# One ring of four PSUM banks, and loads, conversions and products moved, in attention with two MLPs

## The chip, the cores and the metric

The kernel runs on one core of one Trainium2 chip. The metric is the time of one execution in device microseconds, the median of several runs. TensorE (PE) multiplies, VectorE (DVE), ScalarE (ACT) and GpSimd (POOL) work on tiles in SBUF, and the first two of these also read and write PSUM, where TensorE leaves its products. SyncE (SP) issues DMA transfers. Every engine works through its own list of instructions in order and waits where an input is not there yet.

## The reference

```python
def _attn_ref(x, state):                    # x (8, 8, 512, 64), state (8, 8, 32, 64)
    scores = scale * np.matmul(x, state.transpose(0, 1, 3, 2))
    a = softmax(scores); xread = np.matmul(a, state)
    scores2 = scale * np.matmul(state, x.transpose(0, 1, 3, 2))
    a2 = softmax(scores2); sread = np.matmul(a2, x)
    return np.concatenate([xread, sread], axis=2)

x = attn_out.transpose(0, 2, 1, 3).reshape(8 * 544, 512)
h = x @ w_in;  x = (np.maximum(h, 0.0) + alpha * np.minimum(h, 0.0)) @ w_out   # 512 -> 2048 -> 512
h = x @ w2_in; x = (h - np.tanh(h)) @ w2_out                                   # 512 -> 2048 -> 512
```

The softmax is written out here as one word. The weights arrive as 64-bit floats. All products are to be of about single precision.

## The kernel before, in words

**Precision.** A number is kept as two parts of type `fp32r`, a high one and the rest, and each product is made of three matmuls (`TERMS`: high by high, high by low, low by high). The 64-bit weights of the first MLP are turned into such pairs on the chip by a conversion in 32 jobs (`jobs`), each of 128 rows by 512 columns. A job (f, 0) is two slices of 128 columns of `w_in`, and (f, 1) a slice of `w_out`. It passes through steps `conv_load`, `conv_a`, `conv_b`, `conv_s`, `conv_c` and `conv_d`, each a fixed number of ticks after the one before: ScalarE takes the words apart (L112, L124) and makes the high part, VectorE clamps, shifts and masks (L115, L117, L120), GpSimd adds and subtracts (L167, L173, L176).

**Blocks and visits.** The first MLP goes through the tokens in blocks: eight batches of 512 and one of 256 for all state rows. A visit (i, f) is one slice f of 128 of the 2048 hidden units for block i. It makes the hidden product (`emit_h`, tile `ps_h`), the activation (`act_a`, `act_b`: ScalarE, VectorE, ScalarE, VectorE), and then the output product of the visit before (`emit_o`, four accumulators in the pool `ps_acc`). The visits run (0, 0) to (0, 7), then (1, 0) to (1, 15), then (0, 8) to (0, 15), then the blocks from 2 on, with 16 each; the state rows' block (8) comes next to last, before block 7. The first visits run while the weights are still being converted.

**What stands between.** A table, `plan`, puts everything else at one of five places in a visit: `early` (after the hidden product), `gap`, `mid` (after the activation), `late` (after the output product), `end`. Such entries are the attention of the next blocks in steps `s0` to `s6` (transposes `ps_xt`, scores `ps_s`, their softmax, the second transposes `ps_e`, reads `ps_r`, `ps_w`), the turning of states (`ps_st`), the conversion (`conv_step_a`, `conv_step_b`, set by `halves`), and, for blocks from 1 on, the state products (`project_one`, tile `ps_p`).

**State products.** From block 1 on the attention's read is not made as such; the state rows are multiplied by `w_in` ahead, and the hidden product multiplies that by the attention weights. `project_one(b, q, g, p)` does it for two neighbouring blocks at once, for a quarter q of the hidden units, half g of the heads and pair p. It copies the two parts to SBUF, from there to DRAM (`pw_dram`, L416), and `load_parts` (L423) brings each block's rows back as `PW`, for which block 1 uses room in the last piece of `WO`, which is not converted until later.

**PSUM.** There are eight banks: four for `ps_acc`, two for `ps_h` and two for `ps_a`, from which all other tiles come. A pool gives out the bank that was freed first, and its new user waits until the old one has been read.

**The second MLP** is a fast matrix scheme with seven products per pair of slices. An `octet` makes 14 products of six matmuls for two slices (L820); their copies and sums go through small tiles, and `store_g` (L808) sends the results to DRAM. `tasks` lists the block pairs and the order of the weight chunks, of which `load_chunk` (L714) fetches seven at a time and `load_pair` (L726) the next pair's inputs. Banks come from `bank()`, in turn over all eight. The second half (L1001) multiplies the results by the output weights.

The DMA issues mostly stand in SP's list, in the order in which the code calls them.

Of the kernel before, what the change touches and what calls it, by code (L numbers as in the profile page):

```python
# [22 lines left out]
P = 128  # L23
# [12 lines left out]
def attention_and_two_mlps(ctx, tc, x, state, w1_in, w1_out, alpha, w2_in, w2_out, out):  # L36
# [22 lines left out]
    ps_acc = ctx.enter_context(tc.tile_pool(name="ps_acc", bufs=4, space=PSUM))  # L59
    ps_h = ctx.enter_context(tc.tile_pool(name="ps_h", bufs=2, space=PSUM))  # L60
    ps_a = ctx.enter_context(tc.tile_pool(name="ps_a", bufs=2, space=PSUM))
    dram = ctx.enter_context(tc.tile_pool(name="dram", bufs=1, space=DRAM))
# [63 lines left out]

    jobs = [(f, half) for f in range(NF // 2) for half in range(2)]
    jobs += [(f, 0) for f in range(8, 12)] + [(8, 1)] + [(f, 0) for f in range(12, 16)] + [(f, 1) for f in range(9, NF)]
    raws, words, low, loaded = {}, {}, {}, set()
# [179 lines left out]

    def queue(b, g):  # L310
        return nc.scalar if (b, g) == (0, 1) else nc.sync

    def load_state(b, g, tag="sg"):
        sg = work.tile([P, D], F32, tag=tag, name=f"{tag}{b}_{g}", bufs=4)
        queue(b, g).dma_start(out=sg, in_=state[b, g * GH:(g + 1) * GH].rearrange("h n d -> (h n) d"))
        SG[(b, g) if tag == "sg" else (b, g, 0)] = sg

    def load_x(b, g):
        if b < 2:
            load_state(b, g)  # L320
        if b == 0:
            if g == 0:
                xraw[b] = w_outs.tile([P, 2 * NC * GH * D], F32, tag="wo", name="xr0")
            n = NC * GH * D
            t = xraw[b][:, g * n:(g + 1) * n].rearrange("p (c h d) -> p c h d", c=NC, h=GH)
        else:
            t = work.tile([P, NC, GH, D], F32, tag="xr", name=f"xr{b}_{g}")
        for h in range(GH):
            queue(b, g).dma_start(out=t[:, :, h, :],
                              in_=x[b, g * GH + h].rearrange("(p c) d -> p c d", c=NC))  # L330
        xraw[b, g] = t
# [43 lines left out]
    def parts_tile(b, q, g):  # L375
        if b == 1 and q < 2:
            open_wo(NF // FQ - 1)
            t = WO[NF // FQ - 1][:, :, 2 * q + g, :]
        else:
            t = work.tile([P, 2, DM], F32R, tag="raw", name="pw", bufs=4)  # L380
        PW[b, q, g] = [t[:, 0], t[:, 1]]
        return t
# [5 lines left out]
    def staged(b):  # L388
# [6 lines left out]
        n_staged[0] += 1  # L395
        if k < 8:
            open_wi(NF // FQ - 1)
            return tuple(WI[NF // FQ - 1][:, i, k % NCC, :] for i in range(2))
# [4 lines left out]
    def project_one(b, q, g, p):  # L403
# [5 lines left out]
        for k, (i, j) in enumerate(TERMS):  # L409
            nc.tensor.matmul(ps, lhsT=SN[b, g][:, i, cols, :].rearrange("p k m -> p (k m)"),  # L410
                             rhs=WI[q][:, j, g * NP + p, :], start=(k == 0), stop=(k == 2))
        hi, lo = staged(b)
        nc.scalar.copy(hi[d], ps)
        nc.vector.tensor_tensor(lo[d], ps, hi[d].bitcast(F32), op=ALU.subtract)
        for k, t in enumerate((hi, lo)):
            nc.sync.dma_start(out=pw_dram[b, q, g][p, k, d], in_=t[d].bitcast(F32))  # L416
# [178 lines left out]
    def emit_h(blk, n, f):  # L595
        ps = ps_h.tile([P, S], F32, tag="h", name="ps_h")
        if 0 < blk < B:
# [122 lines left out]
    RX, XT = {}, {}  # L720

    def load_pair(u):
        for k in range(2):
            for m in range(2):
                t = slots.get([P, 2, S], F32, f"rx{u}_{k}{m}")
                nc.sync.dma_start(out=t, in_=y_dram[2 * u + m][2 * k:2 * k + 2].rearrange("c p n -> p c n"))  # L726
                RX[u, k, m] = t

# [69 lines left out]
    def bank(shape=(P, S)):  # L798

        pool, tag = ((ps_a, "a"), (ps_a, "a"), *[(ps_acc, "acc")] * 4, (ps_h, "h"), (ps_h, "h"))[turn[0] % 8]  # L800
        turn[0] += 1
        return pool.tile(list(shape), F32, tag=tag, name="ps_m")
# [232 lines left out]
    def timetable(i, a, c):  # L1035

        if i == 0:
            when = dict(s0=(2, "late"), s1=(3, "early"), s2=(3, "late"), s2t=(3, "end"), s2b=(3, "end"), s3=(3, "end"),
                        s3x=(4, "gap"), s3b=(4, "late"), s4=(4, "end"), s4m=(4, "end"), s4t=(4, "end"), s4b=(5, "gap"),
                        s5=(5, "early"), s6=6)  # L1040
            then = dict(s0=(5, "late"), s1=(6, "early"), s2=6, s2t=(6, "late"), s2b=(6, "late"), s3=(6, "late"),
                        s3x=(6, "end"), s3b=7, s4=(7, "early"), s4m=(7, "early"), s4t=(7, "gap"), s4b=7, s5=(7, "late"),
                        s6=(NF, "late"))
        else:
# [5 lines left out]
            start = 7 if i + 2 < B else 5  # L1050
            when, then = (table(0), table(start)) if i > 1 else (table(9), table(8 + NF))
        for g, table in ((a, when), (c, then)):
# [9 lines left out]
    with tc.manual_schedule():  # L1062
# [16 lines left out]
        for f in range(NF // 2):  # L1079
            halves(0, f, "early", "gap")  # L1080
        for f in range(11):
            if f in (2, 3, 4):
                halves(1, f, "early", "gap", "mid", "end")
            else:
                halves(1, f, "gap", "end")
        at(0, 0, "gap", a.s2b)
        at(0, 0, "late", c.s2b)
        at(0, 1, "mid", a.s3b, c.s3b)
# [4 lines left out]
        turns = [(0, 1, 0, (0, "mid"), (1, "late")), (0, 2, 0, (1, "late"), (2, "early")),  # L1093
                 (0, 1, 1, (3, "mid"), (4, "early")), (0, 2, 1, (3, "late"), (4, "late"))]
        for i in (2, 4, 6):
# [17 lines left out]
        todo = [(1, q, g) for q in range(NF // FQ) for g in range(NG)]  # L1113
        places = [(0, 4), (0, 5), (1, 0), (1, 1), (1, 3), (1, 4), (1, 6), (1, 7)]
        todo += [(b, q, g) for b in (3, 5, 7) for g in range(NG) for q in range(NF // FQ)]
# [15 lines left out]
        for i, (blk, n) in enumerate(seq):  # L1131
            if i + 1 < B:
                timetable(i, a, attention(i + 1, 1))
                if i + 2 < B:
                    a = attention(i + 2, 0)
                    for j, f in (((1, 2), (1, 4)), ((0, 9), (0, 15)))[i] if i < 2 else ((i, 6), (i, 13)):
                        at(j, f, "late", load_next_x)
# [85 lines left out]
        for i in range(7):  # L1223
            load_chunk(1, i)
        at_visit = 0
        for k, (u, os) in enumerate(tasks):
            coming = tasks[k + 1][0] if k + 1 < len(tasks) else None
# [99 lines left out]
```

## Time and profile before

| | |
|---|---|
| median of 3 runs | 1509.73 us (1509.43 to 1513.57) |
| the profiled execution | 1510.44 us, span of its instructions 1508.6 us |
| TensorE busy | 1422.1 us, 94% |
| VectorE busy | 991.6 us, 66% |
| ScalarE, GpSimd busy | 729.7 us (48%), 532.1 us (35%) |

Shares are means over stages that are limited by different things: conversion, attention and first visits up to 209 us, the rest of the first MLP up to 815 us, the second MLP's first half up to 1196 us and its second half. Times in rows count from the span's start.

### The profile page before, as it was taken

The numbers are of one execution on the slowest core, as the hardware profiler recorded it, in microseconds if no ns is written. First come the engines' busy times: TensorE is split into PE (matmuls) and PEld (weight loads), VectorE is DVE, ScalarE is ACT, GpSimd is POOL, SyncE is SP. The second block draws the span as 40 slices with busy tenths as digits, with TensorE's granted clock in tenths as the row PEclk, the third lists the DMA queues.
The fourth block names the chain that finished last, engine by engine and source line by source line (L and its number), as shares of the span: only waits on it lengthen the run. The fifth ranks groups of instructions, "written<-read, shape, count | busy, mean of one in ns | idle before, by whom it ended". The sixth has DMA issues, their size and how long they took to land. (4 is left out here: it accounts for less than half of the span.)

```text
span 1508.6 us, 22873 instructions
## 1 busy us (share of the span) xinstructions
PE 1422.1 (94%) x8188; PEld 1192.1 (79%) x8188; DVE 991.6 (66%) x1430; ACT 729.7 (48%) x1322; POOL 532.1 (35%) x414
## 2 busy tenths in 40 slices
PE   5868899999899999999999899999999999999998
PEld 2656687677677677778887787887988999999998
DVE  6879855556577667676345555646347798788874
ACT  3656543444565555555334444545345444444443
POOL 2545400000254444445200222212016486666662
PEclk9998999999999999999999999999999999999999
DMA  5458628795688587749864666272795834444321
GB/s 150 137 163 253 206 80 286 268 300 129 188 213 238 156 247 225 239 158 298 237 209 151 253 202 247 103 272 105 276 346 205 324 133 141 133 141 140 133 85 36
DMA packets 230979, 294.41 MB, mean 195 GB/s; under 512 B 57809, under 2 KB 133585, under 8 KB 229841
## 3 DMA queue, kind: packets, MB, share of 16 engines
q1 hardware_dynamic: 228608, 292.39, 60.2%
q8 instruction: 64, 1.05, 0.3%
q10 hardware_dynamic: 2256, 0.56, 0.2%
q14 instruction: 51, 0.41, 0.1%
HBM read 170.73 MB, written 122.16 MB: 194 GB/s over the span
## 5 line engine op out<-in xcount | busy, mean ns | idle before, releaser
L633 PE MATMUL acc<-g,wo 128*128 128x512 f32 (+1 forms) x1728 | 416.2, 388 | 20.8 <-ACT g L614 11.8
L633 PEld LDWEIGHTS acc<-g,wo 128*128 128x128 f32 x1728 | 312.2, 191 | 104.0 <-ACT g L614 16.6
L1001 PE MATMUL ps_m<-wp,s 128*128 128x256 f32 x2856 | 343.5, 283 | 2.1 <-ACT e L984 2.0
L1001 PEld LDWEIGHTS ps_m<-wp,s 128*128 128x128 f32 x2856 | 342.5, 191 | 3.2 <-ACT e L984 2.2
L820 PE MATMUL ps_m<-x,ch 128*128 128x512 f32 x1344 | 312.7, 394 | 8.6 <-DVE c L837 4.5
L820 PEld LDWEIGHTS ps_m<-x,ch 128*128 128x128 f32 x1344 | 251.7, 188 | 69.0 <-DVE c L837 6.5
L946 DVE TENSOR_TENSOR s<-gt,s 128x512 fp32r<-128x512 f32 (+1 forms) x216 | 220.5, 1072 | 45.4 <-ACT s L962 44.4
L613 DVE SCALAR_TENSOR_TENSOR ps_h<-ps_h,sign,t 128x512 f32<-128x512 f32 (+1 forms) x144 | 104.7, 727 | 144.9 <-ACT t L612 144.4
L614 ACT ACTIVATE g<-ps_h,sign 128x512 fp32r<-128x512 f32 (+1 forms) x144 | 95.8, 666 | 160.5 <-DVE ps_h L613 160.5
L962 ACT CAST s<-gt 128x512 fp32r<-128x512 f32 (+1 forms) x216 | 120.3, 597 | 90.9 <-PE ps_m L1001 37.5
L605 PE MATMUL ps_h<-x,pw 128*128 128x512 f32 x624 | 162.7, 396 | 0.9 <-DMA pw<-pw 0.9
L618 DVE SCALAR_TENSOR_TENSOR g<-ps_h,sign,g 128x512 fp32r<-128x512 f32 (+1 forms) x144 | 102.6, 713 | 62.1 <-ACT g L614 58.9
L612 ACT ACTIVATE t<-ps_h,slope 128x512 f32<-128x512 f32 (+1 forms) x144 | 95.7, 664 | 88.3 <-PE ps_h L605 88.0
L605 PEld LDWEIGHTS ps_h<-x,pw 128*128 128x128 f32 x624 | 114.4, 188 | 26.1 <-issue 1.3
L237 POOL TENSOR_TENSOR c_q<-c_m,c_q 128x512 int32<-128x512 int32 x32 | 42.2, 1319 | 262.3 <-ACT c_q L124 213.0
L831 POOL TENSOR_TENSOR t<-c,t 128x512 f32<-128x512 f32 x32 | 41.7, 1303 | 252.1 <-ACT t L830 239.9
L830 ACT ACTIVATE t<-c 128x512 f32<-128x512 f32 x96 | 60.5, 632 | 123.2 <-DVE c L837 110.3
L837 DVE TENSOR_TENSOR c<-ps_m,c 128x512 f32<-128x512 f32 x96 | 64.7, 685 | 58.9 <-PE ps_m L820 43.2
L264 POOL TENSOR_TENSOR c_o<-c_q,c_o 128x512 fp32r<-128x512 f32 (+1 forms) x48 | 54.4, 1134 | 109.6 <-ACT c_o L262 109.6
L831 DVE TENSOR_TENSOR t<-c,t 128x512 f32<-128x512 f32 x64 | 53.9, 843 | 46.6 <-ACT t L830 46.6
L928 POOL TENSOR_TENSOR s<-gt,gt 128x512 f32<-128x512 f32 (+1 forms) x36 | 53.5, 1492 | 83.2 <-DMA gt<-g 81.5
L167 POOL TENSOR_TENSOR cq<-cm,cq 128x512 int32<-128x512 int32 x32 | 42.0, 1313 | 95.7 <-DVE cm L120 60.5
(138 smaller groups left out, 1663.0 us busy)
## 6 DMA issues: line engine op xcount, KB each, us to landing
g<-t SPq DMA_DIRECT2D x128, 256.0 KB, 2.3
gt<-g SPq DMA_DIRECT2D x64, 512.0 KB, 4.9
wc<-c_o SPq DMA_DIRECT2D x112, 256.0 KB, 3.4
ch<-wc SPq DMA_DIRECT2D x56, 512.0 KB, 7.6
pw<-pw SPq DMA_DIRECT2D x104, 256.0 KB, 5.1
wp<-wc SPq DMA_DIRECT2D x28, 512.0 KB, 7.6
raw<-in_moe_w_in SPq DMA_DIRECT2D x16, 512.0 KB, 4.6
raw<-in_moe_w_out SPq DMA_DIRECT2D x16, 512.0 KB, 4.8
```

Source lines behind the costliest of these rows:

```text
L605: nc.tensor.matmul(ps[:, :n], lhsT=w[i], rhs=xt[:, j, :n], start=(k == 0 and m == 0), stop=(k == len(pairs) - 1 and m == 2))
L612: nc.scalar.mul(t, ph, slope[:, f:f + 1])
L613: nc.vector.scalar_tensor_tensor(ph, ph, sign[:, f:f + 1], t, op0=ALU.mult, op1=ALU.max)
L614: nc.scalar.mul(g[:, 0, :n], ph, sign[:, f:f + 1])
L618: nc.vector.scalar_tensor_tensor(g[:, 1, :n], ph, sign[:, f:f + 1], g[:, 0, :n].bitcast(F32), op0=ALU.mult, op1=ALU.subtract)
L633: nc.tensor.matmul(acc[t][:, :n], lhsT=w[i][:, t * P:(t + 1) * P], rhs=g[:, j, :n], start=(first and k == 0), stop=(last and k == 2))
L820: nc.tensor.matmul(b, lhsT=w[p][:, cc], rhs=XT[key, i][cc][:, q], start=(i not in GOES_ON and cc == k == 0), stop=(cc == 1 and k == 2), sk ...
L831: eng.tensor_tensor(t, h, t, op=ALU.subtract)
L837: nc.vector.tensor_tensor(h, ps[j, i], h, op=ALU.add)
L946: nc.vector.tensor_tensor(made[k - 1][:, 1], src, made[k - 1][:, 0].bitcast(F32), op=ALU.subtract)
L962: nc.scalar.copy(made[k][:, 0], source(blk, i, jj))
L1001: nc.tensor.matmul(dst[:, t * HW:(t + 1) * HW], lhsT=s[:, p, r, t * P:(t + 1) * P], rhs=w[:, q], start=first, stop=(jj == NJ // 2 - 1 and ...
```

## The change

There are six edits.

- `ps_h` and `ps_a` become one pool of four banks, from which hidden products and all other tiles are given out.
- The order of the conversion's jobs: the weights of `w_in` for slice f now come before those of `w_out` for slice f - 1; the last jobs end with slices 12 and 13. The double steps of the conversion in block 1 move from visits 2, 3 and 4 to 5 and 12, and the last steps to 12 and 13.
- The state products for block 1 stay on the chip. The first pair's product is written straight into the tile `PW`; from the second pair's, the rows of block 1 are copied over by DMA from SBUF to SBUF. Only the rows of block 2 go to DRAM. `load_parts` for block 1 is gone.
- Places: some steps of the attention for blocks 1 and 2, some state turns, the state products of block 1, and loads of x.
- The first loads of the second half of the heads go out from SP's list and not from ScalarE's.
- In the second MLP, `load_pair` for the next task, and seven chunks in the first task, are issued one by one after every second product.

```diff
-    ps_h = ctx.enter_context(tc.tile_pool(name="ps_h", bufs=2, space=PSUM))
-    ps_a = ctx.enter_context(tc.tile_pool(name="ps_a", bufs=2, space=PSUM))
+    ps_a = ctx.enter_context(tc.tile_pool(name="ps_a", bufs=4, space=PSUM))
...
-    jobs = [(f, half) for f in range(NF // 2) for half in range(2)]
-    jobs += [(f, 0) for f in range(8, 12)] + [(8, 1)] + [(f, 0) for f in range(12, 16)] + [(f, 1) for f in range(9, NF)]
+    jobs = [(0, 0)] + [j for f in range(1, NF // 2) for j in ((f, 0), (f - 1, 1))] + [(7, 1)]
+    jobs += [(f, 0) for f in range(8, 12)] + [(8, 1)] + [(f, 0) for f in range(12, 16)] + [(f, 1) for f in (9, 10, 11, 14, 15, 12, 13)]
...
-        return nc.scalar if (b, g) == (0, 1) else nc.sync
...
-        if b == 1 and q < 2:
+        if b == 1 and q < 3:
             open_wo(NF // FQ - 1)
-            t = WO[NF // FQ - 1][:, :, 2 * q + g, :]
+            t = WO[NF // FQ - 1][:, :, 2 * (q % 2) + g, :]
...
-        hi, lo = staged(b)
+        if b == 1 and p == 0:
+            parts_tile(b, q, g)
+            hi, lo = PW[b, q, g]
+        else:
+            hi, lo = staged(b)
         nc.scalar.copy(hi[d], ps)
         nc.vector.tensor_tensor(lo[d], ps, hi[d].bitcast(F32), op=ALU.subtract)
+        if b == 1:
+
+            e = slice((1 - p) * HP, (2 - p) * HP)
+            for k, t in enumerate((hi, lo)):
+                nc.sync.dma_start(out=pw_dram[b, q, g][p, k, e], in_=t[e].bitcast(F32))
+            if p:
+                for k, t in enumerate((hi, lo)):
+                    nc.sync.dma_start(out=PW[b, q, g][k][HP:].bitcast(F32), in_=t[HP:].bitcast(F32))
+            return
...
-        ps = ps_h.tile([P, S], F32, tag="h", name="ps_h")
+        ps = ps_a.tile([P, S], F32, tag="a", name="ps_h")
...
-        pool, tag = ((ps_a, "a"), (ps_a, "a"), *[(ps_acc, "acc")] * 4, (ps_h, "h"), (ps_h, "h"))[turn[0] % 8]
+        pool, tag = (*[(ps_a, "a")] * 4, *[(ps_acc, "acc")] * 4)[turn[0] % 8]
...
-            then = dict(s0=(5, "late"), s1=(6, "early"), s2=6, s2t=(6, "late"), s2b=(6, "late"), s3=(6, "late"),
-                        s3x=(6, "end"), s3b=7, s4=(7, "early"), s4m=(7, "early"), s4t=(7, "gap"), s4b=7, s5=(7, "late"),
+                        s3x=(6, "end"), s3b=(7, "early"), s4=(7, "early"), s4m=(7, "early"), s4t=(7, "gap"), s4b=7, s5=(7, "late"),
...
-        for f in range(11):
-            if f in (2, 3, 4):
+        for f in (*range(10), 12, 13):
+            if f in (5, 12):
                 halves(1, f, "early", "gap", "mid", "end")
...
-        places = [(0, 4), (0, 5), (1, 0), (1, 1), (1, 3), (1, 4), (1, 6), (1, 7)]
+        places = [(0, 5), (0, 6), (1, 0), (1, 1), (1, 4), (1, 5), (1, 8), (1, 9)]
...
-        for q, (i, f, place) in enumerate(((0, 7, "early"), (1, 2, "late"), (1, 6, "early"), (1, 9, "early"))):
-            at(i, f, place, partial(load_parts, 1, q))
...
-                load_pair(coming)
+
+                loads.extend(partial(load_pair_part, coming, h, m) for h in range(2) for m in range(2))
             if k == 0:
-                for i in range(7):
-                    load_chunk(2, i)
+                loads.extend(partial(load_chunk, 2, i) for i in range(7))
...
                 def between(n):
+                    if loads and n % 2:
+                        loads.popleft()()
```

The rows that follow show where the edits put instructions. First TensorE's list from visit (0, 4) on; `ps_h` is a hidden product, `acc` an output product, `ps_p` a state product, `ps_e` a transpose of exponentials, `ps_st` a turned state. Before:

```order
L605 MATMUL ps_h<-x_0_3_378,wi_666 128x512 x3
L361 MATMUL ps_st<-ident,sm 128x128
L410 MATMUL ps_p<-wi_342,snp 128x512 x3
L633 MATMUL acc<-g,wo_367 128x512 x12
L361 MATMUL ps_st<-ident,sm 128x128
L410 MATMUL ps_p<-wi_342,snp 128x512 x3
L528 MATMUL ps_e<-ident,e_750 128x128 x4
```

And of the change, in the same visit:

```order
L614 MATMUL ps_h<-x_0_3_374,wi_579 128x512 x3
L357 MATMUL ps_st<-ident,sm 128x128 x2
L642 MATMUL acc<-g,wo_389 128x512 x12
L537 MATMUL ps_e<-ident,e_746 128x128 x4
```

The two state products leave this visit for the next one, and both turned states stand ahead of the output product.

SP's list at the state products of visits (1, 0) and (1, 1); `raw` is a load of 64-bit weights, `pw_1_0` and `pw_1_1` the room in DRAM, `wo` the tile of `PW`, `wi` the staging tile, `y` the finished half of block 0. Before:

```order
L416 DMA pw_1_0_107<-wi_805 128x512 x4
L587 DMA xs<-xw 128x2x32
L667 DMA y_81<-y 128x512 x4
L103 DMA raw_1236<-in_moe_w_in 128x4x256
L416 DMA pw_1_1_108<-wi_805 128x512 x4
L109 DMA raw_1289<-in_moe_w_out 128x1024
L109 DMA raw_1307<-in_moe_w_out 128x1024
L423 DMA wo_1069<-pw_1_0_107 64x2x512 x2
L423 DMA wo_1069<-pw_1_1_108 64x2x512 x2
```

And of the change:

```order
L419 DMA pw_1_0_104<-wo_903 64x512 x2
L419 DMA pw_1_0_104<-wi_924 64x512 x2
L422 DMA wo_903<-wi_924 64x512 x2
L596 DMA xs<-xw 128x2x32
L676 DMA y_78<-y 128x512 x4
L102 DMA raw_1235<-in_moe_w_in 128x4x256
L419 DMA pw_1_1_105<-wo_903 64x512 x2
L419 DMA pw_1_1_105<-wi_924 64x512 x2
L422 DMA wo_903<-wi_924 64x512 x2
```

The stores have half the rows, the copy into `wo` comes from the staging tile and stands right behind them, and no load from DRAM follows behind two raw loads.

SP's list in the first task of the second MLP; `rx` is a part of the next pair's input, `ch` a weight chunk, `g` the room of the results. Before (the row of the last chunk of the seven, and what follows):

```order
L714 DMA ch_6_7747<-wc_2_99 128x2x512
L808 DMA g_0_0_149<-t_01_7832 128x512
L808 DMA g_0_0_149<-t_01_7851 128x512
L808 DMA g_1_0_153<-t_11_7862 128x512
L808 DMA g_0_0_141<-t_00_7874 128x512
L808 DMA g_1_0_153<-t_11_7885 128x512
```

And of the change:

```order
L733 DMA rx_00_7741<-y_80 128x2x512
L733 DMA rx_01_7783<-y_81 128x2x512
L820 DMA g_0_0_146<-t_01_7801 128x512
L733 DMA rx_10_7805<-y_80 128x2x512
L820 DMA g_0_0_146<-t_01_7822 128x512
L733 DMA rx_11_7826<-y_81 128x2x512
```

Four input loads and seven chunk loads stood ahead of the first result; now they stand between the results.

## Rows read from the trace of the kernel before

**Rows 1.** Part 1 of the page: busy time, share of the span, instructions.

```profile
PE 1422.1 (94%) x8188; PEld 1192.1 (79%) x8188; DVE 991.6 (66%) x1430; ACT 729.7 (48%) x1322; POOL 532.1 (35%) x414
```

**Rows 2.** Stretches: length, busy time of PE, PEld, DVE, ACT, POOL, granted clock, DMA share.

```profile
29.30:114.00 84.70, 62.98 (x369) 46.20 (x368) 69.69 (x124) 51.81 (x99) 44.43 (x34) 0.90 0.51 152
114.00:209.00 95.00, 85.64 (x378) 65.69 (x379) 77.54 (x112) 53.84 (x95) 36.89 (x28) 0.93 0.60 181
209.00:815.00 606.00, 580.14 (x3019) 456.89 (x3018) 363.11 (x615) 296.52 (x533) 166.75 (x161) 0.99 0.71 216
815.00:1196.00 381.00, 372.45 (x1852) 311.94 (x1851) 216.75 (x294) 178.92 (x319) 84.31 (x56) 1.00 0.67 240
```

**Rows 3.** TensorE's waits, 29.3 to 209 us: us in total, times, longest.

```profile
PE ps_h L605 <- DMA wo<-pw: 5.2, 4, 3.9
PE ps_xt L460 <- DVE wi L414: 4.1, 1, 4.1
PE ps_r L558 <- ACT e2t L530: 3.9, 1, 3.9
PE ps_h L605 <- POOL wi L173: 3.5, 1, 3.5
PE ps_p L410 <- DVE wi L414: 3.2, 1, 3.2
...
PE ps_st L361 <- ACT e2t L530: 2.2, 1, 2.2
```

**Rows 4.** TensorE's waits, 209 to 815 us.

```profile
PE acc L633 <- ACT g L614: 11.8, 12, 2.9
...
PE ps_p L410 <- DVE pl L414: 3.2, 3, 2.7
PE ps_st L361 <- ACT e2t L530: 2.6, 2, 1.3
```

**Rows 5.** Timeline of TensorE, two hidden products: start, duration, instructions.

```profile
78.83 3.05 PE L605 MATMUL ps_h<-x,wi 128*128 128x512 f32 x12
...
93.14 4.66 PE L605 MATMUL ps_h<-x,wi 128*128 128x512 f32 x12
```

**Rows 6.** VectorE's conversion instructions, 29.3 to 209 us: busy, mean ns, idle before.

```profile
L117 DVE TENSOR_SCALAR cm<-cm 128x512 int32<-128x512 int32 x30 | 28.4, 947 | 1.0
L120 DVE SCALAR_TENSOR_TENSOR cm<-raw,cm 128x512 int32<-128x512 int32 x30 | 23.1, 772 | 0.3
L115 DVE TENSOR_SCALAR cm<-cm 128x512 f32<-128x512 f32 x29 | 19.4, 670 | 0.3 <-ACT cm L112 0.3
```

**Rows 7.** Stretches as in rows 2, two shorter ones.

```profile
29.30:66.20 36.90, 29.84 (x174) 21.60 (x172) 32.46 (x59) 24.53 (x46) 22.51 (x18) 0.87 0.50 147
...
114.00:148.00 34.00, 29.23 (x102) 21.96 (x103) 32.01 (x45) 21.20 (x37) 17.41 (x14) 0.80 0.85 243
```

**Rows 8.** Timeline of ScalarE at the copy of a state product.

```profile
293.07 0.59 ACT L413 CAST ph<-ps_p 128x512 fp32r<-128x512 f32 x1 [5.48 <-DMA pw<-ph]
```

**Rows 9.** Line 117, 114 to 148 us: duration in ns, least, median, greatest.

```profile
L117 DVE TENSOR_SCALAR cm<-cm x8: 426/1375/1404, 116.3 to 147.4; 128x512 int32<-128x512 int32 x8
```

**Rows 10.** Timeline at the first task of the second MLP.

```profile
824.19 9.15 SPq L714 DMA_DIRECT2D ch<-wc  x7
...
834.30 25.64 SPq L808 DMA_DIRECT2D g<-t  x13
...
845.04 1.56 ACT L826 COPY c<-ps_m 128x512 f32<-128x512 f32 x3 [6.59 <-DMA g<-t]
845.68 11.17 PE L820 MATMUL ps_m<-x,ch 128*128 128x512 f32 x48 [2.57 <-ACT c L826]
```

**Rows 11.** Timeline at the start.

```profile
4.63 0.40 SPq L103 DMA_DIRECT2D raw<-in_moe_w_in  x1
...
8.55 1.09 PE L460 MATMUL ps_xt<-ident,xr 128*128 128x128 f32 x4 [0.80 <-ACT e L465]
...
20.25 1.20 ACT L112 ACTIVATE cm<-raw 128x512 f32<-128x512 f32 x2
```

More of the change, by code (lines that the diff above doesn't have):

```diff
@@ L308, in attention_and_two_mlps @@
     xraw, SG = {}, {}
-    def queue(b, g):
-        return nc.scalar if (b, g) == (0, 1) else nc.sync
     def load_state(b, g, tag="sg"):
         sg = work.tile([P, D], F32, tag=tag, name=f"{tag}{b}_{g}", bufs=4)
-        queue(b, g).dma_start(out=sg, in_=state[b, g * GH:(g + 1) * GH].rearrange("h n d -> (h n) d"))
+        nc.sync.dma_start(out=sg, in_=state[b, g * GH:(g + 1) * GH].rearrange("h n d -> (h n) d"))
         SG[(b, g) if tag == "sg" else (b, g, 0)] = sg
@@ L328, in load_x @@
         for h in range(GH):
-            queue(b, g).dma_start(out=t[:, :, h, :],
+            nc.sync.dma_start(out=t[:, :, h, :],
                               in_=x[b, g * GH + h].rearrange("(p c) d -> p c d", c=NC))
@@ L395, in staged @@
         n_staged[0] += 1
-        if k < 8:
+        if k < 4:
             open_wi(NF // FQ - 1)
@@ L720, in attention_and_two_mlps, with load_pair_part @@
     RX, XT = {}, {}
+    def load_pair_part(u, k, m):
+        t = slots.get([P, 2, S], F32, f"rx{u}_{k}{m}")
+        nc.sync.dma_start(out=t, in_=y_dram[2 * u + m][2 * k:2 * k + 2].rearrange("c p n -> p c n"))
+        RX[u, k, m] = t
     def load_pair(u):
@@ L724, in load_pair @@
             for m in range(2):
-                t = slots.get([P, 2, S], F32, f"rx{u}_{k}{m}")
-                nc.sync.dma_start(out=t, in_=y_dram[2 * u + m][2 * k:2 * k + 2].rearrange("c p n -> p c n"))
-                RX[u, k, m] = t
+                load_pair_part(u, k, m)
     def split_to(o, src):
@@ L1037, in timetable @@
         if i == 0:
-            when = dict(s0=(2, "late"), s1=(3, "early"), s2=(3, "late"), s2t=(3, "end"), s2b=(3, "end"), s3=(3, "end"),
+            when = dict(s0=(3, "early"), s1=(3, "gap"), s2=(3, "late"), s2t=(3, "end"), s2b=(3, "end"), s3=(3, "end"),
                         s3x=(4, "gap"), s3b=(4, "late"), s4=(4, "end"), s4m=(4, "end"), s4t=(4, "end"), s4b=(5, "gap"),
@@ L1050, in timetable @@
             start = 7 if i + 2 < B else 5
-            when, then = (table(0), table(start)) if i > 1 else (table(9), table(8 + NF))
+            when, then = (table(0), table(start)) if i > 1 else ({**table(9), "s0": (10, "early"), "s1": (10, "late")}, table(8 + NF))
         for g, table in ((a, when), (c, then)):
@@ L1087, in attention_and_two_mlps @@
         at(0, 0, "late", c.s2b)
-        at(0, 1, "mid", a.s3b, c.s3b)
+        at(0, 1, "mid", a.s3b)
+        at(0, 1, "late", c.s3b)
         at(0, 2, "mid", a.s5)
@@ L1092, in attention_and_two_mlps @@
         a = attention(1, 0)
-        turns = [(0, 1, 0, (0, "mid"), (1, "late")), (0, 2, 0, (1, "late"), (2, "early")),
-                 (0, 1, 1, (3, "mid"), (4, "early")), (0, 2, 1, (3, "late"), (4, "late"))]
+        turns = [(0, 1, 0, (0, "mid"), (2, "early")), (0, 2, 0, (1, "late"), (2, "gap")),
+                 (0, 1, 1, (3, "mid"), (4, "early")), (0, 2, 1, (3, "late"), (4, "mid"))]
         for i in (2, 4, 6):
@@ L1135, in attention_and_two_mlps @@
                     a = attention(i + 2, 0)
-                    for j, f in (((1, 2), (1, 4)), ((0, 9), (0, 15)))[i] if i < 2 else ((i, 6), (i, 13)):
+                    for j, f in (((1, 4), (1, 10)), ((0, 9), (0, 15)))[i] if i < 2 else ((i, 6), (i, 13)):
                         at(j, f, "late", load_next_x)
@@ L1225, in attention_and_two_mlps @@
         at_visit = 0
+        loads = deque()
         for k, (u, os) in enumerate(tasks):
```

## The prediction

> **What bounds the kernel now.** I began with the shares of the page: TensorE is busy for 94% of the span [rows 1], so 86.5 us (1508.6 less 1422.1) are all that fewer waits can give, plus what a slow clock costs. Then a table of stages, to see where those 86.5 us lie [rows 2]: of the 179.7 us between 29.3 and 209 (the first 24 visits) TensorE idles 31.1 (21.7 and 9.4); of the 606 us of the rest of the first MLP it idles 25.9; of the 381 us of the second MLP's first half 8.6. The second half of the second MLP is touched by no edit.
>
> Then the waits of TensorE by stage. In the first 24 visits [rows 3] no one engine holds it. 5.2 us are hidden products for block 1 that wait for their weights, which go out to DRAM and come back. 9.5 us (4.1, 3.2 and 2.2) are waits for a bank of `ps_a`: a transpose or a state product that may not start before the tile two places earlier in that ring of two has been copied out. 3.9 us are `s5` behind a copy that stands late in ScalarE's queue, 3.5 us the second visit behind its converted weights. After 209 [rows 4] the ring of two costs 5.8 us (3.2 and 2.6), and 11.8 us are waits for the activation itself, which this change leaves alone.
>
> A stop costs more than its length. Twelve matmuls of a hidden product take 3.05 us at 78.83 and 4.66 us at 93.14, right behind the stop of 4.13 us [rows 5]: the granted clock has gone to its lower level, and it comes back while they run. So a stop of this kind costs 1.6 us on top. The mean clock of 0.90 over 84.7 us and 0.93 over 95 us [rows 2] is 8.5 + 6.7 = 15.2 us of full-speed time lost in the first 24 visits, if TensorE had work for all of it.
>
> **What limits the gain there.** TensorE could win up to 31.1 + 15.2 = 46 us, if VectorE let it. VectorE is busy 69.69 + 77.54 = 147.2 us of those 179.7 [rows 2], 82%. A conversion step costs it 70.9 us in 30 steps (28.4 + 23.1 + 19.4), 2.4 us each [rows 6], and none is removed. So I cost the first 24 visits by VectorE's rate and not by TensorE's waits. In two stretches where it was itself the limit, it reached 32.46 of 36.9 us (88%) and 32.01 of 34 (94%) [rows 7].
>
> **The change, part by part.**
>
> *Ring of four.* A transpose or a state product now takes the bank of the tile four places back in a joint ring, not two; while the scores tile `ps_s` is held, three back, not one. The 9.5 us of rows 3 go; what is late next is the activation on VectorE, in order. After 209 the 5.8 us go too, and with the stop of 2.7 us one fall of the clock (1.6): 7.4 at most. But the largest of them stood behind a ScalarE copy that itself waited 5.48 us for a DMA store to free its staging tile [rows 8]. That wait stays, and the activation of the next visit is queued behind it. I take 5, between 2 and 7.4.
>
> *Products kept on chip.* For each of 8 product pairs four stores of 256 KB and two loads of 256 KB become four stores of half that and two copies of 128 KB inside SBUF: 1.5 MB become 0.75. The hidden product of (1,4) no longer waits for the way through DRAM, the 3.9 us within the 5.2 of rows 3, and its clock fall of 1.6 us. ScalarE and VectorE do what they did. The new copies are issued in SP's queue behind the wait for their product; behind them stand raw weight loads, needed a step later. If the first store is slow, the copy over the same rows waits for it: a wait on SP, two visits (some 12 us, as 16 visits fill the 95) before the weights are read.
>
> *Conversions.* Visit 1's weights come one step earlier, which is the 3.5 us wait; its place is taken by the activation of visit 0, which VectorE reaches no sooner. The doubled steps leave (1,2) to (1,4) for (1,5) and (1,12): by the end of (1,4) there are 5 steps instead of 8, so 3 x 2.4 = 7.1 us of VectorE's work leave the stretch in which it was at 94%, for one with room (the 95 us window as a whole is at 82%).
>
> *Attention places.* The copy before `s5` now stands ahead of the activation of visit 7: the 3.9 us shrink; the x parts behind them still wait for VectorE.
>
> All four meet on VectorE. At 90%, between its two rates, 69.69 us need 77.4 instead of 84.7 and 77.54 need 86.2 instead of 95: 7.3 + 8.8 = 16.1 us. Bounds: at 85%, barely above today, 2.7 + 3.8 = 6.5; at 95%, 11.3 + 13.4 = 24.7. I take 16.1, near the measured pair.
>
> One rule speaks against this. Rows first: the conversion's shift-and-mask takes 426 ns at the least and 1375 at the median between 114 and 148 [rows 9], on equal tiles. The Trainium skill ("SBUF — State Buffer", Who interferes with whom) says that VectorE and GpSimd share one port pair under an exclusive lock, and that such an instruction blocks until the other's ends; the spread agrees. By it, packing the same work tighter puts more of it beside GpSimd's and makes VectorE's 147 us grow. By the rows VectorE's work stays at 147.2 and the gain is 16.1; the rule's outcome is the second case below.
>
> *Loads between products.* Eleven loads of 512 KB were issued at once; 13 result stores behind them took SP 25.64 us to issue, ScalarE sat 6.59 us without a free tile and TensorE 2.57 [rows 10]. Now one load goes out after every second product, so a store has at most one new load ahead. I take 2.6, and as the lower bound 0. If the loads came late: the pair is wanted an octet later, the chunks two octets later, and an octet is 84 matmuls.
>
> *First loads.* Group 1's five loads go from ScalarE's queue to SP's. The weights behind them are issued some 3 us later, having been issued at 4.63 and first read at 20.25: covered. ScalarE starts free of issuing, and the second transpose stops 0.80 us less at most [rows 11]. I take 0.8, between 0 and 0.8.
>
> **Sum** against the profiled execution's own 1510.44 us (0.7 above the median of the runs, 1509.73): 16.1 + 5 + 2.6 + 0.8 = 24.5, so **1486 us**. Lower bounds of the gain 6.5 + 2 + 0 + 0 = 8.5 give 1502, upper ones 24.7 + 7.4 + 2.6 + 0.8 = 35.5 give 1475.
>
> **Rivals.**
>
> *VectorE absorbs the early gain.* Same order on each engine, but less idle time beside GpSimd: if half of the 59 conversion instructions of the first and second kind rose from their mean (670 and 947 ns) to the 1375 of rows 9, that is 30 x 0.57 = 17 us, and the 16.1 are gone. For it: rows 9, and the same number of steps. (It is the case that the rule of the Trainium skill's "SBUF — State Buffer", Who interferes with whom, would bring about.) Against: three steps move to where VectorE has room. The rest, 5 + 2.6 + 0.8, less what shrinks too, gives 1500 to 1505.
>
> *The change doesn't reach the end.* The copies on chip stand behind SP's waits, the hidden products of block 1 still wait, and the ring only moves the stop from a product to the activation: 1506 to 1513. For it: the 11.8 us of activation waits [rows 4] stay. Against: at least two of the stops are for banks that are empty.
>
> *Slower: hidden products behind products.* The hidden product had two banks of its own. Now, with `ps_s` held, its next bank can be the one that the same visit's first state product has just left; in the built program that is so in five of the 24 visits with two products. Should that copy wait for a store as in rows 8 (5.48 us), the hidden product, its activation and the visit start later. Five times 5.48 is 27.4 us, less 24.5: 1513; it decides from 4.9 us each. With a fall of the clock at each (1.6) it is 35.4: 1521. Against: all waits of products for a copy from 209 to 815 come to 3.2 us in three [rows 4].
>
> **Chances.** Forecast (1476 to 1494) 0.60; VectorE absorbs (1494 to 1505) 0.26; no effect 0.08; slower 0.06. About 0.3%, 4.5 us, is what a measurement of this kernel can tell from no change. The first two lie beyond it on the fast side but for a little: faster 0.85, same 0.09, slower 0.06. The range 1476 to 1502 holds the forecast and more than half of the second case; some 0.2 is left out.
>
> **What would show it.** Right: no wait of a transpose or product for the ring of two, no wait of block 1's hidden products for a weight DMA, VectorE near 90% between 29 and 209 and that stretch some 16 us shorter, the clock near 1.0 there; no ScalarE wait for result stores near the second MLP's start. Wrong: VectorE's conversion instructions longer in the mean than 947 and 670 ns (second case); `ps_h` waiting for VectorE's parts of `ps_p` between 209 and 370 us (slower). The prediction fails by its early term alone if that stretch shrinks by under 7 us or over 25.

## The result, and the profile after

The changed kernel takes 1493.58 us (median of 4 runs, 1488.67 to 1495.53) against 1510.13 us before: ratio 0.9881, 95% interval 0.9851 to 0.9911. The profiled execution has a span of 1493.2 us, 15.4 less than before. The forecast was 1486 us, a gain of 24.5.

Part 1 of the page after, to set beside [rows 1]:

```profile
PE 1418.0 (95%) x8188; PEld 1191.7 (80%) x8188; DVE 988.2 (66%) x1430; ACT 728.8 (49%) x1322; POOL 533.8 (36%) x414
```

The engines execute as many instructions as before. Of the 15.4 us TensorE's idle time gave 11.3 (86.5 before, 75.2 after) and its matmuls 4.1 (2.2 of them in the first 24 visits, where the granted clock rose). Stretches of the kernel after, cut where the same work begins (first hidden product, first of block 1, first of block 0's second half, second MLP, its second half); columns as in [rows 2]:

```profile
27.66:105.28 77.62, 60.27 (x370) 44.32 (x368) 67.05 (x118) 48.35 (x93) 42.26 (x32) 0.93 0.51 142
105.28:202.11 96.83, 86.02 (x383) 65.50 (x378) 75.33 (x116) 56.38 (x100) 39.27 (x30) 0.95 0.47 131
202.11:801.67 599.56, 577.96 (x3017) 458.08 (x3016) 362.79 (x614) 296.00 (x533) 166.51 (x161) 0.99 0.72 219
801.67:1142.90 341.23, 334.88 (x1537) 274.77 (x1536) 191.19 (x265) 162.98 (x290) 71.51 (x47) 1.00 0.64 230
```

Cut at the same work, before has 29.37, 84.64, 94.89, 605.86 and 343.75 us. So the start gave 1.7 us, the first two stretches 7.0 and -1.9, the rest of the first MLP 6.3, the second MLP's first half 2.5; the last part took 0.2 back. The first 24 visits together shrank by 5.1 us, where 16.1 were forecast: these 11.0 us are more than the whole miss of 9.1, and the other stages gave 1.9 us more than forecast. VectorE was to be busy 90% of that time; it is 67.05 + 75.33 = 142.4 of 174.45 us, 82%, as before. The granted clock was to be near 1.0 there; it went from 0.90 and 0.93 to 0.93 and 0.95.

TensorE's waits between 27.66 and 202.11 after, beside [rows 3] (us in total, times, longest):

```profile
PE ps_h L614 <- DVE g L627: 4.4, 3, 3.8
PE ps_e L537 <- ACT e L519: 4.2, 2, 3.4
PE acc L642 <- DVE g L627: 3.3, 3, 1.9
PE ps_xt L469 <- DVE wide L577: 2.9, 1, 2.9
PE ps_h L614 <- ACT x L336: 2.8, 1, 2.8
PE acc L642 <- ACT g L623: 2.8, 2, 1.7
PE ps_h L614 <- DVE snp L369: 2.5, 1, 2.5
```

Of the stops in [rows 3] only that of `s5` (`ps_r`) is left, with 1.8 us; no hidden product waits for a DMA, none for GpSimd's weights. Others stand in their place. The three largest of one kind are waits for a bank of the joint ring that VectorE has not yet left: 4.4 and 2.5 us of hidden products (`ps_h`, which needs neither `g` of the visit before nor `snp`) and 2.9 us of a transpose (`ps_xt`), 9.8 us together. In sum TensorE idles 28.2 us in these visits, against 31.1 before: some 20 us of the stops of [rows 3] are gone, and some 17 us of others have come. A stop that moved by one place, in TensorE's timeline before, and then after:

```profile
37.85 3.92 PE L605 MATMUL ps_h<-x,wi 128*128 128x512 f32 x10 [3.48 <-POOL wi L173]
```

```profile
37.59 0.66 PE L537 MATMUL ps_e<-ident,e 128*128 128x128 f32 x4 [3.44 <-ACT e L519]
```

Before, the stop was for the second visit's weights. They are there now; the next thing in its list is a transpose whose input ScalarE has not yet made.

One stop was made by the change. Timelines of SP, ScalarE and VectorE after, and then SP's own wait ahead of the copy (us in total, times, longest):

```profile
124.19 1.29 SPq L419 DMA_DIRECT2D pw<-wo  x2
125.58 1.21 SPq L419 DMA_DIRECT2D pw<-wi  x2
130.51 1.11 SPq L422 DMA_DIRECT2D wo<-wi  x2
...
132.91 0.62 ACT L163 CAST wi<-cm 128x512 fp32r<-128x512 f32 x1 [4.78 <-DMA wo<-wi]
...
134.15 0.76 DVE L622 SCALAR_TENSOR_TENSOR ps_h<-ps_h,sign,t 128x512 f32<-128x512 f32 x1 [4.13 <-ACT t L621]
```

```profile
SPq L422 <- DMA pw<-wo: 3.6, 1, 3.6
```

Read the timelines from the bottom: VectorE waits for the activation, which stands behind a conversion on ScalarE, which may not write the fourth slice's `w_in` while a product staged in that tile is still to be copied over; and that copy waited in SP's list until the store of 124.19, which reads the same rows of `PW`, had landed.

### The profile page after: what moved, and what is told of

It reads as the page before. It is cut to its first block, busy times and chain, and to the rows that moved or that the text cites. A ratio compares the mean times of both kernels' runs of the same rounds, so it can differ in the third digit from the quotient of the medians.

```text
span 1493.2 us, 22867 instructions
## 1 busy us (share of the span) xinstructions
PE 1418.0 (95%) x8188; PEld 1191.7 (80%) x8188; DVE 988.2 (66%) x1430; ACT 728.8 (49%) x1322; POOL 533.8 (36%) x414
## 4 chain that ended last, share of the span: by engine, by line
PE 70%; DVE 8%; DMA 6%; ACT 4%; issue 3%; SPq 1%; POOL 1%; DVEq 0%; ACTq 0%; POOLq 0%
PE ps_m L1013 21%; PE ps_m L832 17%; PE acc L642 16%; PE ps_h L614 9%; PE ps_p L406 2%; DVE ps_h L622 2%; PE ps_m L897 2%; DVE g L627 2%; DMA gt<-g 1%; DMA c_raw<-in_moe_w_in 1%; ACT g L623 1%; ACT t L621 1%; DMA g<-t 1%; DVE c L849 1%; PE ps_s L503 1%
## 5 line engine op out<-in xcount | busy, mean ns | idle before, releaser
L642 PE MATMUL acc<-g,wo 128*128 128x512 f32 (+1 forms) x1728 | 420.7, 391 | 24.1 <-ACT g L623 14.8
L614 PE MATMUL ps_h<-x,pw 128*128 128x512 f32 x600 | 156.9, 397 | 0.0
L614 PEld LDWEIGHTS ps_h<-x,pw 128*128 128x128 f32 x600 | 111.0, 189 | 24.2
L166 POOL TENSOR_TENSOR cq<-cm,cq 128x512 int32<-128x512 int32 x32 | 41.9, 1311 | 102.3 <-DVE cm L119 64.7
```

The source lines that it names most:

```text
L614: nc.tensor.matmul(ps[:, :n], lhsT=w[i], rhs=xt[:, j, :n], start=(k == 0 and m == 0), stop=(k == len(pairs) - 1 and m == 2))
L642: nc.tensor.matmul(acc[t][:, :n], lhsT=w[i][:, t * P:(t + 1) * P], rhs=g[:, j, :n], start=(first and k == 0), stop=(last and k == 2))
```

## The experiments

Twelve kernels. e1, e2, e5, e6, e8, e9 and e10 are made from the changed kernel, e3, e4, e7, e11 and e12 from the one before. Ratios are to the kernel before as measured beside each (1509.0 to 1510.6 us). e6 and e10 compute other values and e8 leaves a limit out: they show where time goes and are no kernels to use. "Stretch" is from the first hidden product to the first of block 0's second half, "late" from there to the second MLP, "VectorE" its busy time in the stretch.

| kernel | median us | ratio to before (95%) | stretch | VectorE | late |
|---|---|---|---|---|---|
| before | 1510 | | 179.5 | 147.1 | 605.9 |
| after | 1493.6 | 0.9881 (0.9851 to 0.9911) | 174.5 | 142.4 | 599.6 |
| e1 after, one staging place moved | 1487.7 | 0.9845 (0.9826 to 0.9863) | 171.2 | 144.6 | 599.5 |
| e2 after, two rings of two | 1509.8 | 0.9997 (0.9986 to 1.0008) | 185.9 | 141.4 | 602.6 |
| e3 before, ring of four | 1495.5 | 0.9893 (0.9876 to 0.9911) | 173.6 | 146.8 | 596.1 |
| e4 before, start and second MLP's loads | 1503.7 | 0.9952 (0.9936 to 0.9968) | 181.1 | 145.1 | 603.5 |
| e5 after, products through DRAM | 1493.3 | 0.9881 (0.9863 to 0.9900) | 177.5 | 141.6 | 597.8 |
| e6 e1, old conversions | 1497.8 | 0.9913 (0.9898 to 0.9929) | 177.7 | 147.1 | 598.4 |
| e7 e3 and e4 together | 1491.8 | 0.9876 (0.9860 to 0.9892) | 172.6 | 146.3 | 597.6 |
| e8 e1 without the clamp | 1468.2 | 0.9720 (0.9703 to 0.9738) | 159.8 | 119.7 | 590.4 |
| e9 e1, old places | 1487.5 | 0.9855 (0.9831 to 0.9880) | 169.9 | 143.7 | 598.7 |
| e10 e1 without GpSimd's add | 1480.5 | 0.9805 (0.9787 to 0.9822) | 161.7 | 128.7 | 597.5 |
| e11 e7, new order of first jobs | 1493.2 | 0.9877 (0.9856 to 0.9898) | 172.7 | 147.2 | 601.3 |
| e12 e7, new places | 1494.8 | 0.9897 (0.9880 to 0.9914) | 177.9 | 147.5 | 597.3 |

Parts that no edit touches differ by some us between single profiles (late: 602.6 to 605.9 with two rings, 596.1 to 601.3 with one), so differences of 1 or 2 us there say nothing. The stretch, too, is that of one execution each: before and e4, and e3 and e7, have the same instructions in it and differ by 1.5 and 1.0 us.

**e1: the copy's staging place.**

```diff
-        if k < 4:
+        if k < 3:
...
-        ... for t in (("e2", "e2t"), ("sc", "at"))[k % 2])
+        ... for t in (("e2", "e2t"), ("sc", "at"))[k != 3 and k % 2])
```

> The changed kernel, with one staging place moved: the lower product of the fourth pair for block 1 is staged in the pair of attention tiles e2, e2t and no longer in the tile of the fourth slice's first-layer weights. In the changed kernel's trace ScalarE stands 4.78 us (127.5 to 132.9) before it may write those weights, because the copy inside SBUF out of the staging place starts only at 130.51. Theory C (that copy is what ate the gain of the second stretch, 105.3 to 202.1 us): the stop goes, the stretch shrinks from 96.8 us to 92 to 93, the time is 4 to 5 us below the changed kernel, near 1489. Theory V (VectorE is the limit there whatever ScalarE does, as the prediction's second case has it): the stop goes, VectorE fills the place, the stretch stays within 1 us and the time within 1.5 us of the changed kernel.

ScalarE goes through the place without a stop:

```profile
127.12 0.68 ACT L123 ACTIVATE cq<-raw 128x512 int32<-128x512 uint32 x1
127.68 0.63 ACT L163 CAST wi<-cm 128x512 fp32r<-128x512 f32 x1
```

Its second stretch is 93.6 us instead of 96.8, the span 3.8 and the median 5.9 us shorter. That is theory C, a little short of it in the stretch: the stop cost 3 to 4 us net, and VectorE did not eat them.

**e2 and e3: the ring undone, and the ring alone.** e2 gives `ps_h` and the rest two banks each again and deals `bank()` as before; e3 is the opposite edit on the kernel before:

```diff
-    ps_h = ctx.enter_context(tc.tile_pool(name="ps_h", bufs=2, space=PSUM))
-    ps_a = ctx.enter_context(tc.tile_pool(name="ps_a", bufs=2, space=PSUM))
+    ps_a = ctx.enter_context(tc.tile_pool(name="ps_a", bufs=4, space=PSUM))
```

> The changed kernel with the ring undone: two banks for hidden products and two for the rest, all else as changed. By the prediction's terms 5 us (2 to 7.4) come back in 202 to 802 us and some 5 to 9 before it: 1504 to 1508. Theory R (the joint ring makes early waits of its own: 11.1 us of TensorE's waits between 27.7 and 105.3 are for a bank that VectorE has not yet left, the largest a hidden product of 3.8 us behind the activation of the visit before): early the two layouts cost about the same, within 3 us, and only the later stretch pays: 1496 to 1501.

> The kernel before with the ring of four alone. By the prediction's terms: 5 us less in 209 to 815 us, and most of the 9.5 us of bank waits before 209, so 1496 to 1500. Theory R: the late 5 to 6 us and within 3 us of nothing early: 1502 to 1508. If the shared ring is the slower rival's (hidden products behind products), early stretch longer than 179.5 us and 1506 or more.

On e2 the loss is larger than either theory had it; on e3 the time lies half a us below what the prediction's terms gave, the early part is 5.9 us, and R falls. The ring alone brings 14.6 us, and all else without it nothing (ratio 0.9997). In the stretch it gives 5.9 us on the old rest and 11.4 on the new. TensorE's waits of e2 there:

```profile
PE ps_r L568 <- DVE snp L370: 4.2, 1, 4.2
PE ps_xt L470 <- DVE wo L415: 4.1, 1, 4.1
PE ps_s L504 <- DVE wo L415: 4.0, 1, 4.0
PE ps_p L407 <- DVE wide L578: 3.6, 1, 3.6
...
PE ps_w L593 <- DVE xw L596: 2.8, 1, 2.8
```

The five lines are stops for a bank two places back, 18.7 us; with the ring of four the three groups above come to 9.8. The joint ring does make hidden products wait, but for less than it saves.

**e4: start and second MLP alone** (loads of the next task one after every second product; group (0, 1) loaded from SP).

> The kernel before with the loads between products and the first loads on SP's queue alone; no edit between 29 and 815 us. By the prediction 2.6 + 0.8 = 3.4 us less; by the stages of the changed kernel's trace 2.5 + 1.7 = 4.2 us less: 1505.9 to 1506.7. If the start's gain is taken back by VectorE, 2.5 us: 1507.6.

It gained 6.4 us by the median, more than any of the three forecasts; by its stages 3.0 at the start and 3.3 in the second MLP, and the stretch did not take them back beyond 1.5. (Another 2.4 us lie in the late stretch, which it leaves alone.) Timelines of ScalarE and TensorE at the start, and the issues of the first x from the DMA view (0 to 12 us), with KB each and the median us to landing. Before:

```profile
3.85 1.28 ACT L484 ACT_TABLE_LOAD   x1 [3.85 <-issue]
...
6.66 1.09 PE L460 MATMUL ps_xt<-ident,xr 128*128 128x128 f32 x4 [2.56 <-DMA xr<-in_x]
```

```profile
xr<-in_x SPq DMA_DIRECT2D x4, 128.0 KB, 4.5
```

And e4:

```profile
0.73 1.28 ACT L484 ACT_TABLE_LOAD   x1 [0.73 <-PEq L1316]
...
5.26 2.26 PE L460 MATMUL ps_xt<-ident,xr 128*128 128x128 f32 x8 [1.43 <-DMA xr<-in_x]
```

```profile
xr<-in_x SPq DMA_DIRECT2D x8, 128.0 KB, 3.0
```

Before, with two queues, the first group's four loads landed 4.5 us (median) after their issue; now the eight loads of both groups take 3.0. ScalarE began its table load at 3.85 us before, behind five DMA issues. The first transposes begin 1.4 us sooner. The forecast counted one stop of 0.80 us behind ScalarE [rows 11] and not that the first group's data come sooner. That stop was hardly ScalarE's alone: in e3, whose start is that of the kernel before, the same transposes wait for the load,

```profile
8.74 1.11 PE L459 MATMUL ps_xt<-ident,xr 128*128 128x128 f32 x4 [0.77 <-DMA xr<-in_x]
```

**e5, e6: products through DRAM, and old conversions, each put back alone.**

> The changed kernel with block 1's state products through DRAM again (all staged, two loads a pair, at the places of the kernel before); ring, conversions and attention places as changed. The prediction took 5.2 us of waits and 1.6 us of slow clock off with the products kept on chip, and priced the copies inside SBUF at nothing; so this one would be 6.8 us slower than the changed kernel, 1498 to 1502, with hidden products waiting for a DMA of their weights. Theory C (the copies cost 4.8 us of ScalarE's time at the fourth slice's weights and so some 4 us of the stretch): that stop is absent here, and the two ways differ by 2 to 3 us only: 1495 to 1497.

> The kernel of e1 with the conversions as in the kernel before: first-layer weights of a slice together with its second-layer weights, doubled steps at (1,2) to (1,4). By the prediction the wait for the second visit's weights (3.5 us there, 2.4 in e3) comes back and 7.1 us of VectorE's work fall where it had no room: 3 to 8 us slower than e1, 1491 to 1496. Theory A (the ring and the two edits outside the first 24 visits are the whole gain; the order of the conversions only moves work about): within 2 us of e1, 1486 to 1490.

e5 equals the changed kernel by its median, below both ranges; its stretch is 3.0 us longer, as theory C had the difference. e6 (1497.8) lies above both of its ranges. In e6, hidden products of block 1 read tiles that already hold later `w_out` slices, so its values differ and 2.5 of its waits are its own. TensorE's waits of e5 and then of e6 in the stretch:

```profile
PE ps_h L601 <- DMA wo<-pw: 8.8, 4, 4.2
```

```profile
PE ps_h L614 <- POOL wi L172: 3.8, 2, 3.6
...
PE ps_h L614 <- ACT wo L165: 2.5, 3, 1.6
```

The waits named in the forecast return with the old parts: the DMA's, and larger than the 5.2 us of [rows 3], and the weights' with 3.8. Against e1 the stretch is 6.3 and 6.5 us longer, e6's own 2.5 included.

**e7: ring, start and second MLP together**, on the kernel before.

> The kernel before with the ring of four, the loads between products and the first loads on SP's queue; conversions, products and attention places as before. If the measured parts add up (14.6 us of e3 and 6.4 of e4 off 1510.1): 1489. Theory A: 1487 to 1491, no worse than the whole change at 1493.6. By the prediction, where conversions, products and places carry more than half of the early 16.1 us: at least 5 us slower than e1, 1493 or more.

It takes 1491.8 us, the changed kernel's time, without the new conversions, products and places. The two measured parts nearly add up (18.8 us of 21.0). So in the changed kernel the other three edits bring nothing together, which e5 and e6 seemed to contradict. With the staging place moved (e1) they bring 1.4 us of the stretch; the median is 4 us lower, but the intervals of the two ratios still touch.

**e9, e11, e12: one edit at a time.** e9 puts the old tables (attention, state turns, loads of x) back into e1, e12 the new ones into e7; e11 changes one line of e7:

```diff
-    jobs = [(f, half) for f in range(NF // 2) for half in range(2)]
+    jobs = [(0, 0)] + [j for f in range(1, NF // 2) for j in ((f, 0), (f - 1, 1))] + [(7, 1)]
```

> The kernel of e1 with the attention and state places of the kernel before; ring, conversions and products on chip stay. Against e1, the old conversions cost 6.5 us and products through DRAM 6.3 us of the stretch before the second half of block 0, yet e7, which has both old and the old places too, is only 1.4 us longer there. Theory P (the new places cost what the other two bring): without them the stretch is 5 us or more shorter than e1's 171.2 and the time 1480 to 1484. Theory I (the three belong together, each pays only with the others): the stretch is 2 to 7 us longer than e1's and the time 1489 to 1495, with the wait of s5 behind its copy (3.9 us) back.

> The kernel of e7 with the first conversions' new order alone (first-layer weights a slice ahead); doubled steps, products and places as before. By the prediction, the wait of the second visit for its weights (2.6 us in e7) goes, and nothing else is late: 1488 to 1490. Theory I (each of the three pays only with the others): VectorE gives the 2.6 us back, 1490.5 to 1493.

> The kernel of e7 with the new attention and state places alone (old conversions, products through DRAM). e5 and e6 put one of these two back into a kernel with the new places and lost 6.3 and 6.5 us of the stretch against e1, while e7, with both back and the old places, lost 1.4. Theory M (the new places come later for the states, so they hurt the old products and conversions, and these two only make that good): the stretch is 176 us or longer where e7 has 172.6, and the time 1494 to 1500. Theory X (places are free with either, as e9 has it for the new products; e5 and e6 lose for another reason): within 1.5 us of e7, 1490 to 1493.5.

e9 met neither theory: the old places bring the long wait of `s5` back and still cost nothing (169.9 us against 171.2). e12 meets theory M: the new places make the old parts' stretch 5.3 us longer, and the median 3.0. TensorE's waits of e9, then e12, then e11, and last e7:

```profile
PE ps_r L567 <- ACT e2t L539: 6.2, 2, 5.1
```

```profile
PE ps_h L604 <- DMA wo<-pw: 9.1, 4, 3.8
PE ps_h L604 <- DVE g L617: 3.9, 1, 3.9
PE ps_h L604 <- POOL wi L172: 3.6, 1, 3.6
```

```profile
PE ps_e L527 <- ACT e L509: 4.7, 2, 3.7
```

```profile
PE ps_h L604 <- DMA wo<-pw: 4.2, 3, 3.3
...
PE ps_h L604 <- POOL wi L172: 2.6, 1, 2.6
```

In e12 the states are turned later, and block 1's weights come back later from DRAM: 9.1 us of waits where e7 has 4.2. The new products and conversions make this good and little more, and only together: with the new places, e5 (177.5 us) and e6 (177.7) have one of the two each and are no shorter than e12 (177.9), and e1 has both and is 6.7 us shorter. In each of e5 and e6 the stop of the part that stayed old remains. In e11 the weights' wait is gone, and the transposes behind it wait 4.7 us instead (as at 37.59 above): they begin 9.9 us after the first hidden product, where in e7 it is 10.2, and the stretch gains nothing.

**e8, e10: VectorE's load made smaller.** e8 leaves the clamp out (`min`, `max` of L114), e10 the add on GpSimd (L166).

> The kernel of e1 with one of VectorE's three conversion instructions left out, the clamp of the high word (it leaves out the limits on very small and very large weights). In the changed kernel's trace it takes 20.1 us of VectorE's 142.3 between 27.7 and 202.1. Theory V (the stretch is VectorE's work at a constant busy share, as the prediction's sum has it): 171.2 us of e1 shrink by 20.1/0.845 = 24 us at most, and by 15 at least, where TensorE's own 144.7 us of work become the limit: 1464 to 1473. Theory L (the stretch is bound by round trips between VectorE, ScalarE and TensorE in program order, and VectorE's share just follows): only the clamps that stand ahead of an activation or a copy count, 4 to 10 us: 1478 to 1484.

> The kernel of e1 with one of GpSimd's two conversion instructions left out (the sum of high and low word, so the converted low parts hold something else). In e1, VectorE's clamp and its shift-and-mask take 49.6 us in 58 instructions between 27.4 and 198.6, their shortest forms (0.41 and 0.43 us) would make 24.4. Theory S (they are long because they run beside GpSimd): with some 30 of its 60 conversion instructions gone, VectorE's two fall by 8 us or more, to 42 or less, and the stretch by half of that or more, so 1479 to 1484. Theory N (their length has nothing to do with GpSimd): 48 to 51 us as before, and 1486 to 1489.

VectorE's two instructions in the stretch in e1, then in e10:

```profile
L116 DVE TENSOR_SCALAR cm<-cm 128x512 int32<-128x512 int32 x29 | 29.1, 1002 | 1.0
...
L114 DVE TENSOR_SCALAR cm<-cm 128x512 f32<-128x512 f32 x29 | 20.5, 706 | 0.0
```

```profile
L116 DVE TENSOR_SCALAR cm<-cm 128x512 int32<-128x512 int32 x29 | 16.5, 570 | 1.0
L114 DVE TENSOR_SCALAR cm<-cm 128x512 f32<-128x512 f32 x29 | 14.0, 484 | 0.0
```

e10 is theory S: 49.6 us become 30.5. In e1's trace up to the second MLP, the shift-and-masks beside which GpSimd runs nothing (35 of 64) take 429 ns at most, and the other 29 take 1243 on average. By the median e8 lies where theory V put it, but for another reason: its span is 22.4 us shorter than e1's, and 9.1 of these are in the late stretch, where 32 more clamps are left out. In the early stretch 24.9 us less work on VectorE give 11.4 us, 0.46 for one; in e10 15.9 give 9.4, 0.6 for one. The 11.4 us are below the 15 that theory V needs at least and just above the 4 to 10 of theory L: VectorE's work counts for about half.

## Why the prediction was right and wrong, step by step

**Right.** The direction, and that the ring's later part is 5 us: the late stretch averages 604.0 us in the three kernels with two rings and 598.5 in nine with one (e8 and e10 left out); single pairs give 3.0 (e2 and after) to 9.8 us (before and e3). The second MLP: 2.5 us after, and over ten kernels with the edit 341.7 us (e8 and e10 left out again) against 343.8 and 343.1 in the two without, 1.7 on average, against 2.6 (single kernels with the edit reach from 340.5 to 343.2). In the first task ScalarE no longer waits for a result store as in [rows 10].

**Too small: the first loads.** 0.8 forecast, 1.7 after, 3.0 in e4: the data of the first group come sooner, not only ScalarE.

**The step that failed: "All four meet on VectorE", at 90%.** The forecast itself set the test: the early term fails if the stretch shrinks by under 7 us; it shrank by 5.1, less than the 6.5 of its lower bound. That the time still came out within the forecast's first case, by 0.4 us at a spread of the runs of 7, is luck. VectorE's share stayed at 82%, and no kernel here that does all of the work is above 85.2% (e11), where the forecast took 85% as its lower bound. The 88 and 94% of [rows 7] show a busy VectorE in two short stretches, not that it was the limit there. It is not the rate that sets this stretch: with 141.4 us of VectorE's work it took 185.9 us (e2), with 146.8 us 173.6 (e3), and a us less of that work gave half a us (e8, e10). The stretch is a chain in program order between three engines, in which VectorE's idle time is itself a wait for ScalarE, and ScalarE's largest wait is for VectorE (after, us in total, times, longest):

```profile
DVE ps_h L622 <- ACT t L621: 17.6, 12, 4.1
```

```profile
ACT g L623 <- DVE ps_h L622: 34.8, 24, 5.6
```

All waits of VectorE for ScalarE come to 29.3 of its 32.1 us idle. Behind a removed stop stood not VectorE's queue but the next transpose or activation, so most stops moved rather than went.

**The four parts that were to meet, by themselves.** *Ring*: 5.9 us alone in the stretch, 11.4 with the rest; "The 9.5 us of rows 3 go" was wrong in form, since bank waits of the new ring, 9.8 us, stand in their place; that the ring pays all the same is shown by e2 and e3. *Products kept on chip*: the DMA waits went as said, and with the way through DRAM e5 has 8.8 us of them; but "a wait on SP, two visits (some 12 us, as 16 visits fill the 95) before the weights are read" looked at the wrong reader. The late copy holds the staging tile, which is the next weights' place, and cost ScalarE 4.78 us; e1 shows 3 to 4 us net. *Conversions*: the wait went, and by e11 the new order of the first jobs brought nothing alone; the moved double steps were not tried by themselves. *Attention places*: "the 3.9 us shrink", and they did, to 1.8, but the places cost 5.3 us with the old parts and nothing measurable with the new. So the ring carried the change, and the three others, which were to add to it, nearly cancelled.

**The rivals.** "VectorE absorbs": the time after lies half a us below its 1494 to 1505, but its mechanism did not act: conversion instructions took 935, 735 and 693 ns after, against 947, 772 and 670 [rows 6]. The length that it speaks of is real, and was there before: in e10, with half of GpSimd's instructions gone, 19.1 of VectorE's 49.6 us go. The Trainium skill ("SBUF — State Buffer", Who interferes with whom) says that an instruction of this kind (`tensor_scalar`) can run in a mode that needs the ports shared with GpSimd, and then blocks while GpSimd holds them. The 429 ns at most and 1243 on average of e1, and e10, agree. The change did hardly anything to that overlap. "Slower", hidden products behind the ring: they do wait there (4.4 and 2.5 us), behind an activation and a state's copy rather than a product, and e2 shows that the ring pays for it. "No effect" is excluded by the interval.

**What beats both.** e1 (1487.7 us) and e9 (1487.5) have the lowest times with all of the work done, and cannot be told apart. They are faster than before; against the change the ratios' intervals still touch (0.9851 to 0.9863 is in both e1's and its own), and what speaks for the step is the stretch, 3.3 and 4.5 us shorter, and for e1 the stop that is gone.

**Open.** Why the new places cost nothing in e9's company but 5.3 us in e12's is seen only in the DMA waits; that these alone are the cause was not tried. Differences of stretches rest on one profiled execution of each kernel, so the 5.3 us and the sums of parts hold to a us or two.

## What to carry to other kernels

Removing a stop from a chain of engines that work in order is worth, at first, the difference to the next stop behind it, so look up what the waiting engine's list holds next and when its input is ready; a busy share of 82% was no rate here that packing could raise to 90. A tile used for staging belongs to two chains: ask who writes it next, and price the last DMA that reads it at that writer. A joint ring of banks can be worth more than careful placing, and should be measured alone first, since edits made beside it may cost without showing.

## What the runs showed of the hardware

With 31 of GpSimd's 61 instructions of the stretch left out, VectorE's shift-and-mask fell from 1002 to 570 ns on average and its clamp from 706 to 484: an engine that TensorE hardly waits for (0.9 us in e1's stretch) cost VectorE 19 us. In e1, 35 shift-and-masks beside which GpSimd ran nothing took 429 ns at most. At the start, four loads of 128 KB on SP's queue beside four on ScalarE's landed 4.5 us after their issue (median, the kernel before); eight on SP's queue in order took 3.0 (e4). The first weight loads were also issued sooner before, at 4.63 us against 7.19, so what the second queue did by itself is not separated.
